# Six groups of attention outputs turned by VectorE in 32x32 blocks and moved between SBUF quadrants, in place of TensorE's transposes, under a new written order

## The chip, the core and the metric

The kernel runs on one core of a Trainium2 chip. A core has engines that run side by side, each through its own list of instructions, strictly in order: TensorE (PE; its weight loads are listed apart as PEld), VectorE (DVE), ScalarE (ACT), GpSimd (POOL) and SyncE (SP), which here only issues transfers. An engine stops at an instruction whose semaphores are not yet up, and everything behind it in its list stops with it. SBUF is the working memory of 128 partitions (four quadrants of 32), PSUM the small memory that TensorE writes into. The metric is device time in microseconds; lower is better.

## What is computed

The reference is linear attention with a feature map, followed by a soft mixture of experts:

```python
proj = einsum('bhsd,df->bhsf', x, w_phi);  proj -= max(abs(proj), -1)
phi(x) = concat([exp(proj), exp(-proj)], -1)               # 256 features, for q and k
kv, z  = einsum('bhsf,bhsd->bhfd', k_p, v), sum(k_p, 2)
out    = einsum('bhsf,bhfd->bhsd', q_p, kv) / (einsum('bhsf,bhf->bhs', q_p, z) + 1e-6)
# 8 batches x 8 heads x 576 tokens x 64;  x = out as 4608 tokens x 512
logits = x @ phi                                           # 32 slots: 8 experts x 4
d      = softmax of logits over all tokens;   slot_input = d.T @ x
slot_out[e] = relu(slot_input[e] @ w1[e]) @ w2[e]          # w1 512x1024, w2 1024x512, each expert
y      = softmax of logits over slots @ slot_out
```

All is float32. The matrix `x` never goes to memory: its tiles stay in SBUF until their part of `slot_input` has been added up.

## The kernel before, in words

**Attention.** The batches go in four pairs (`bp`), a pair of one head is a unit `u` (32 units of nine tiles of 128 tokens). For four tiles at a time (`b`, 72 of them), `proj` multiplies K and Q by `w_phi` into PSUM; VectorE takes maxima (`kmax`, `qabs`), ScalarE the exponentials (`kneg_exp`, `kpos_exp`, `qpos`, `qneg`), GpSimd scales V (`vals`), and TensorE adds up `kv` (`kvmm`). Then `num` multiplies Q's features with `kv`, three tiles at a time, VectorE combines the two halves (`scale`, `comb`, `recip`) and GpSimd divides (`divide`) into a tile `xc[n]` of 128 tokens x 4 x 512.

**A group.** When all eight heads of a pair are divided, two tiles `xc[n]` are full, n = 0 to 5 for the first three pairs; these are the six groups of the title. For each, the logits need `x` turned so that the 512 features lie on the partitions. Before, TensorE did it: task `turn` is four 128x128 transposes into a PSUM bank (line 741), four such tasks in a group, each followed by `xcopy` (line 745), which copies the bank to SBUF on ScalarE or VectorE, two and two. `logits` (line 424) then multiplies with `phs`. Behind it follow `gmax`, `gexp`, `dturn`, `dcopy`, `slotsum` and `update`, which keep a running softmax over tokens and its sum. The last pair's groups (`fturn`, `fxcopy`, `flogits`) have code of their own and come at the end of attention.

**The order.** All of that is a list of tasks. The string `ORDER` has one letter for each task, in the order in which they are written into the engines' lists; `Plan.run` checks that each task's inputs are written earlier and hands out buffers. No scheduler reorders anything afterwards. A letter's place is no time: two engines meet only where one waits for the other.

**Transfers.** SP issues all of them in one list: `xs` (K and Q, 512 KB, three buffers), `vt` (V, 325 KB, two buffers), and the 64 expert weights `wt` (512 KB each). Where SBUF is not yet needed for attention, weights come early: `room` gives the number of weight slots in each stretch of memory, 30, 33, 39, 42, 43 and 49 before; the first 30 are free from the start, the others come free as pools are closed (`ends`), and the last 15 weights reuse slots. Each transfer counts up one of eight semaphores (DMAHW0 to 7 below), in turn, and the program makes a transfer wait for the one that used its semaphore eight transfers earlier, so at most eight are in flight.

**The tail.** After attention the final groups' tasks (`z...`), the experts' first and second layer (lines 848 and 943) and the combination with the outputs (lines 972 to 976) follow, all by TensorE in a written order.

Of the kernel before, what the change touches and what calls it, by code (L numbers as in the profile page):

```python
# [9 lines left out]
F32 = mybir.dt.float32  # L10
# [6 lines left out]
B, H, S, D = 8, 8, 576, 64  # L17
FE = 128
NBP = B // 2
# [4 lines left out]
G = 4  # L24
# [20 lines left out]
BUFS = {'xs': 3, 'kf': 3, 'vs': 2, 'vt': 2, 'qf': 3, 'un': 2, 'xT': 4, 'xc': 2}  # L45
# [4 lines left out]
def room(bufs):  # L50

    parts = [bufs["xs"] * XW * 4, bufs["kf"] * 4096 + bufs["vs"] * 2624 + bufs["vt"] * 2624,
             bufs["qf"] * 4096 + 2 * 1056 + 512, bufs["un"] * 2368, (bufs["xc"] + 1) * G * DM * 4]
    return [int(n) // 4096 for n in np.cumsum([TOP - bufs["xT"] * 2048 - sum(parts)] + parts)]


class Plan:
# [43 lines left out]
    "abbccdeafdebgbehiejefechigcjdklfmbgdnoelhimjfajkegmhijcpnoclfdmqlrhisgmfjktharujnovmvkbdicnogpcjdwmgwflrjhirqvaw"  # L101
    "mxfysbkrkdtnomlhizvnocAwgpvjcjwflmdqbrAArvkshimnoltfwckvdgnojrwfrgdkyjahimzlhivnocwqvpcgbdjmgdflrAfwAhimsjklnotr"
    "hiyAmkcjvnopgwcjbdavmxgzflArdqjmwlAfaAkvrwhisynorhizmtkgcjnovvjpwcblfxdmAqrwAAfsrkgmvhitlnojwkvchwajnoyrblrdiqmv"
    "vgwkzjcdpwfmdrgynoAsrfjkmhilAathiznoAcgvjcvblfxAwmxqdAAwrgpkjsfmnolhirtvmvkwdnorwghijrvyzmAcpjwvcwAbflxyAhrazfAd"
    "imkAlgBnojdBqcCgCjsBbBdatmlCkvjwrnoChirvgfjmhiDkpAnocEwFvcwkflmbhrxqxdimGgsnojBflBtCaxchCjykdiBnozBgCfjmvhwrClpr"
    "vdimDwgvkjwnocEFcblqadHxHIrJIKksfKnoltLmqyAdAgAhirfjmgkhicpjnovscbfvxtwmlwrzflAhrvAAdimwgvhyjrwkdiajrnozvgkmjvcp"
    "nowwcAblfyhAmzqdirlgmkjsfAahrxtnoxmjkvdicAnovApwAgcGlfjhwmlqrJdirfvgmkwjsknoradnotbchijvywcblfxgvmxqjdrwpdhimvgr"
    "kzwAsmkMgylftrnozLAhiAcnojvcbdjaxwmglfAvrqApjwmkshiArfvtnowmdkMyNvhirwgljrvnojmvczwwpcyAbxlaAzArdkAlmfAnoBhiBgCc"
    "jCfkdBqdBmCgfjshinoajrlxCAbmktDphivvnocwEgwjclfFrbqrvdmwgBsfBkmktCCjdhiBvnoOajBhiyxCcClrwflrnovNzdmkwhiDgnojpcEq"
    "vGwcFblgsHHrItdmyKIjfzlhiKAdkaxALgmAnoqvJrfMjmgvkwhiwAscnoApctblAxdrjGrgvfwmkdhilrgjvajmvkwnoOPfrjNnomvhicwwPpyc"  # L110
    "yzbdkAlmfdgrnojzqJmlAajhixsAfrAOhimtkcnovvpwcgbdjlmgfrwqjdrvAklaAmhixwjnosfchitgmkvbjfxwrlxhrpyvnowmkvczdiAnowqc"
    "dyAAglmfjshirfLatbrkvgmzvkAwnodMrnApjglohicvjqwcwdmsygAfhirtfrPvkjwmaxjkdblgrjlnomzhivcpnoAvwcwAlfyAhmqdirzdgmAN"
    "ksjnoABaxgtbBCjcfCAhivjBwdBCmCrlfplrkvhimvnoDknocEqwcgblFjwBfsBCrtmjkvCwHflBnorIhCrqvJmdiGwBdKCvgwhiDjkgnocEysFc"
    "bpzLxAHaArItlmKdknomAfygjvhirwfzAravkdmlhijOgcnowqApAcvbdjmwgsfrfltrlkPymvhijwhajnoxdirkvmgznovjcGpwcblfAdmqlrks"
    "gmhijwfLAnoarytxhmAkdijcnovvpzgcwAlfjwmqdrdgArAksgmMhivtnowfljcvkyjwrnojlrzJqdmAvkvMcwAnowsgycpAhilNtrQzrAvAwmOR"
    "jlRSmvkPSqwRfRSNhirkTSvsnomUwtORApRSyQrnoVVSRvrSTvwzwARUArASyRPQvzyRwSzWASWWAyTzAXXQXYYUZYZ0WZ001223145367186794"
    "525435985658++-Q++*//=-=<>*!>!!!-*>")
# [15 lines left out]
def tile_kernel(ctx: ExitStack, tc, xT, vv, w, phi, w1, w2, cst, out):  # L133
# [13 lines left out]
    stacks = {k: ExitStack() for k in ("x", "c", "u", "q", "v", "mm", "h", "zl", "num")}  # L147
# [6 lines left out]
    def pool(k, name, **kw):  # L154
        return stacks[k].enter_context(tc.tile_pool(name=name, **kw))
# [10 lines left out]
    xp = pool("x", "xp", bufs=BUFS["xs"], side="right")  # L166

# [253 lines left out]

    def slotmm(ps, kc, t, stop=True):
# [224 lines left out]
    def spin(x):  # L647
# [3 lines left out]
                     kb0=1, kb1=1, qb0=1, qb1=1, pkv=1, kvs=2, psn=2, mo=2, mk=6, mh=1, eq=3, dn=3, lT=3, de=2,  # L651
# [10 lines left out]
    for b in range(NB + 2):  # L662
        def task(kind, engine, cost, fn, key, bank, **k):
            add(kind, key, engine, cost, lambda: fn(key), at=4 / 3 * bank, **k)
# [8 lines left out]
        for p, (b_, u, t0, t1) in enumerate(pieces):  # L673
            if b_ == b:
# [6 lines left out]
                task("kvmm", PE, 0.233 * n + 0.215 * mid, kvmm, p, b, after=[("kpos_exp", b), ("vals", p)] + ([("kvmm", p - 1)] if p else []),  # L681
# [8 lines left out]
    for s in range(NK):  # L690
# [44 lines left out]
        for i, group in enumerate(groups):  # L735
# [17 lines left out]
        def logits(m, xTs=xTs, got=got, groups=groups):  # L753
# [3 lines left out]
        task(f + "logits", PE, 0.225 * len(groups), logits, m, mode="s",  # L757
             after=[(f + "xcopy", (m, i)) for i in range(len(groups))], get=hold("logits", m),
             put=[("xT", (m, i)) for i in range(len(groups))], lat=0.22)
# [43 lines left out]
    ends = [("x", [("proj", NB + 1), ("weight", nslot[0] - 1)]),  # L803
# [7 lines left out]
    last("zopen", 1, None, 0.0, lambda: zopen("r"), after=[("zopen", 0), ("close", 1)], lat=0.0)  # L811
# [238 lines left out]
```

## Time and profile before

| | |
|---|---|
| median of 3 runs | 338.7 us (338.18 to 339.12) |
| the profiled execution | 339.44 us, of which the span from first to last instruction is 337.3 us |
| TensorE | busy 325.8 us (97% of the span) |
| VectorE | 243.8 us (72%) |
| ScalarE | 234.4 us (69%) |
| GpSimd | 168.3 us (50%) |
| transfers | 74.10 MB, 220 GB/s mean |

Attention lasts to about 268 us, the end of the slot sums to 280 us, the experts and outputs to the end. Groups 0 and 1 are turned between 73 and 90 us, 2 and 3 between 137 and 152 us, 4 and 5 between 205 and 216 us. Busy time of matmuls is modelled and overlaps; how much time a stretch of TensorE's work takes is read from the starts in the chain of waits.

### The profile page before, as it was taken

To read this page: it belongs to the slowest core of one execution; us is meant where nothing else is said; L and a number is where in the kernel's file an instruction comes from. 1 tells how busy PE (TensorE), PEld (TensorE's weight loads), DVE (VectorE), ACT (ScalarE), POOL (GpSimd) and SP (SyncE) were. 2 spreads that over 40 slices of the span, in tenths; PEclk is the share of its full clock that TensorE was granted. 3 is DMA by queue.
4 is the path that set the end of the run, shared out by engine and by line. 5 is a ranking of instruction groups with operands and counts; after the bars stand their busy time and mean duration, and the time that the engine had idled before them with its cause. 6 is when DMAs were issued, how large, how long until landed. Compare 5 with 4: busy or idle time off the path is not lost.

```text
span 337.3 us, 16424 instructions
## 1 busy us (share of the span) xinstructions
PE 325.8 (97%) x6955; PEld 274.7 (81%) x6955; DVE 243.8 (72%) x683; ACT 234.4 (69%) x680; POOL 168.3 (50%) x353
## 2 busy tenths in 40 slices
PE   8999999999999999999999999999999999999982
PEld 4899998999979999998899999979998745355750
DVE  1478887786979888778898977778998552716642
ACT  2899988968886996887788987867886241205541
POOL 1645766863547667642877785248593520240000
PEclk9999999999999999999999999999999999999997
DMA  6646366553755784465557845233618859994987
GB/s 232 176 134 227 104 211 226 203 189 117 286 166 166 230 290 172 173 224 164 167 177 253 277 176 183 67 145 127 230 45 309 311 202 386 411 409 194 391 338 301
DMA packets 22409, 74.10 MB, mean 220 GB/s; under 512 B 2496, under 2 KB 2880, under 8 KB 22336
## 3 DMA queue, kind: packets, MB, share of 16 engines
q1 hardware_dynamic: 22336, 73.05, 60.6%
q8 instruction: 55, 0.90, 1.1%
q14 instruction: 18, 0.15, 0.1%
HBM read 63.60 MB, written 9.44 MB: 217 GB/s over the span
## 4 chain that ended last, share of the span: by engine, by line
PE 91%; DVE 4%; ACT 1%; issue 1%; POOL 0%; DVEq 0%; ACTq 0%; POOLq 0%
PE kvp L318 23%; PE psn L371 21%; PE psq L271 12%; PE psk L271 10%; PE hp L848 4%; PE psx L741 4%; PE yp L943 4%; PE psl L424 3%; PE pso L972 2%; PE pss L463 2%; PE psw L190 1%; DVE o L973 1%; PE pss L566 1%; PE psd L456 1%; PE psh L910 1%
## 5 line engine op out<-in xcount | busy, mean ns | idle before, releaser
L291 POOL TENSOR_TENSOR vs<-vt,mk 128x520 f32<-128x520 f32 (+3 forms) x128 | 91.6, 732 | 70.1 <-ACT mk L280 52.3
L318 PE MATMUL kvp<-vs,kf 128*64 128x65 f32 (+1 forms) x2304 | 92.5, 229 | 0.0
L318 PEld LDWEIGHTS kvp<-vs,kf 128*64 128x64 f32 x2304 | 81.5, 138 | 7.1 <-issue 2.3
L371 PE MATMUL psn<-kvs,qf 128*64 128x65 f32 x2304 | 80.3, 223 | 0.7 <-issue 0.6
L371 PEld LDWEIGHTS psn<-kvs,qf 128*64 128x64 f32 x2304 | 73.6, 138 | 3.8 <-issue 1.7
L271 PE MATMUL psq<-xs,wd 64*128 64x128 f32 x576 | 75.8, 280 | 0.1
L271 PE MATMUL psk<-wd,xs 64*128 64x128 f32 x576 | 75.7, 280 | 0.1
L271 PEld LDWEIGHTS psq<-xs,wd 64*128 64x128 f32 x576 | 67.6, 187 | 3.1 <-issue 1.5
L271 PEld LDWEIGHTS psk<-wd,xs 64*128 64x128 f32 x576 | 67.2, 187 | 3.0 <-issue 1.5
L276 DVE TENSOR_REDUCE mk<-psk 128x4 f32<-128x512 f32 x72 | 48.4, 676 | 13.6 <-PE psk L271 8.1
L333 DVE TRANSPOSE_TENSOR_REDUCE mts<-psq 128x16 f32<-128x512 f32 x72 | 50.7, 707 | 6.6 <-PE psk L271 3.6
L302 ACT ACTIVATE kf<-psk 128x512 f32<-128x512 f32 x72 | 42.6, 592 | 17.2 <-DVE mk L276 7.5
L338 ACT ACTIVATE qf<-psq 128x512 f32<-128x512 f32 x72 | 42.4, 594 | 8.0 <-DVE dn L398 2.6
L382 DVE TENSOR_TENSOR un<-psn,eq 128x195 f32<-128x195 f32 x96 | 33.1, 351 | 18.3 <-PE psn L371 9.6
L413 POOL TENSOR_TENSOR xc<-un,dn 128x256 f32<-128x256 f32 x64 | 39.3, 616 | 13.5 <-DVE dn L398 11.0
L341 ACT ACTIVATE qf<-psq 128x512 f32<-128x512 f32 x72 | 43.2, 603 | 0.5 <-DVE mts L333 0.5
L305 ACT ACTIVATE kf<-psk 128x512 f32<-128x512 f32 x72 | 42.5, 596 | 0.5 <-DVE mk L276 0.4
L387 DVE TENSOR_TENSOR un<-psn,un 128x195 f32<-128x195 f32 x96 | 32.9, 349 | 1.0
L349 ACT ACTIVATE mh<-mts 32x36 f32<-32x36 f32 x128 | 29.5, 230 | 5.4 <-DVE mts L333 3.4
L355 DVE TENSOR_REDUCE eq<-mh 32x9 f32<-32x36 f32 x128 | 26.3, 205 | 1.5
L279 ACT ACTIVATE mk<-mk 128x4 f32<-128x4 f32 x72 | 15.1, 210 | 12.4 <-DVE mk L276 10.9
L973 ACT COPY o<-pso 128x512 f32<-128x512 f32 x20 | 11.4, 597 | 8.9 <-PE pso L972 8.9
(130 smaller groups left out, 346.0 us busy)
## 6 DMA issues: line engine op xcount, KB each, us to landing
wt<-w SPq DMA_DIRECT2D x64, 512.0 KB, 5.9
xs<-xT SPq DMA_DIRECT2D x36, 512.0 KB, 4.3
vt<-vv SPq DMA_DIRECT2D x32, 325.0 KB, 3.2
out<-o SPq DMA_DIRECT2D x17, 512.0 KB, 4.2
out<-o SPq DMA_DIRECT2D x2, 256.0 KB, 4.0
xs<-xT SPq DMA_DIRECT2D x2, 128.0 KB, 2.6
cs<-cst SPq DMA_DIRECT2D x1, 128.5 KB, 2.9
wd<-w SPq DMA_DIRECT2D x1, 64.0 KB, 2.1
```

Source lines behind the costliest of these rows:

```text
L271: nc.tensor.matmul(ps, l, r, start=True, stop=True)
L276: nc.vector.tensor_reduce(km[b][:, 2], kx[b], axis=AX, op=ALU.max, apply_absolute_value=True)
L291: nc.gpsimd.tensor_tensor(vs[b][:, :, place(b, u, t, o):place(b, u, t, o) + n], v[:, t + o:t + o + n].unsqueeze(1).broadcast_to([128, 2, n ...
L302: nc.scalar.activation(kf[b][:, 1], kx[b], AF.Exp, scale=-1.0)
L305: nc.scalar.activation(kf[b][:, 0], kx[b], AF.Exp)
L318: nc.tensor.matmul(ps[f:f + FE // 2, pn, o:o + m], kf[b][:, pn, NT * u + t - 4 * b, f:f + FE // 2], v2[:, pn, at:at + m], start=(t == 0 an ...
L333: nc.vector.tensor_reduce(mts.rearrange("p r j -> p j r")[:, o:o + 4], qx[b].rearrange("p j (r t) -> p (j r) t", t=32), axis=AX, op=ALU.ma ...
L338: nc.scalar.activation(qf[b][:, 0], qx[b], AF.Exp)
L341: nc.scalar.activation(qf[b][:, 1], qx[b], AF.Exp, scale=-1.0)
L371: nc.tensor.matmul(ps[64 * f:64 * f + 64, j, pn], q2[:, pn, 64 * f:64 * f + 64], kv[:, pn, b2], start=True, stop=True)
L382: nc.vector.tensor_tensor(un[u][:, CH * c:CH * c + CH], nx[s][:, :, 0], e[:, 1].unsqueeze(2).broadcast_to([128, CH, 65]), op=ALU.mult)
L413: nc.gpsimd.tensor_tensor(x[:, :, h * D:(h + 1) * D], un[u][:, a:b, 0:64], dn[u][:, a:b].unsqueeze(2).broadcast_to([128, b - a, 64]), op=A ...
```

## The change

For groups 0 to 5, `turn` and `xcopy` are replaced by two tasks. `xturn` (four in a group, on VectorE) turns all 32x32 blocks of one 128x512 tile of `xc[n]` and writes them to a tile `yb`, sorted by the quadrant they belong to. `xmove` (four in a group, on SP, each four transfers of 32 partitions x 2 KB = 64 KB) carries quadrant i of `yb` to the free places i of `xTb`, from quadrant i to every quadrant q. Each of the four `xmove` needs all four `xturn`. `logits` reads `xTb` in place of the copied banks. `yb` and `xTb` exist once each: the next group's `xturn` waits until the transfers of this one have read `yb`, and its `xmove` until `logits` has read `xTb`.

The two tiles take 16 KB of each partition, and `xc` has three buffers instead of two (8 KB more), so `room` now gives 24, 28, 31, 37, 40, 41 and 49 weight slots: 24 from the start, four more when the new pool is closed behind group 5. `kvmm` 4 waits for the eight warming matmuls in the list. `ORDER` is new from the first letter to the last. The final groups keep TensorE's transposes.

```diff
-BUFS = {'xs': 3, 'kf': 3, 'vs': 2, 'vt': 2, 'qf': 3, 'un': 2, 'xT': 4, 'xc': 2}
+BUFS = {'xs': 3, 'kf': 3, 'vs': 2, 'vt': 2, 'qf': 3, 'un': 2, 'xT': 4, 'xc': 3}
...
-    parts = [bufs["xs"] * XW * 4, bufs["kf"] * 4096 + bufs["vs"] * 2624 + bufs["vt"] * 2624,
+    parts = [2 * G * DM * 4, bufs["xs"] * XW * 4, bufs["kf"] * 4096 + bufs["vs"] * 2624 + bufs["vt"] * 2624,
...
-    "abbccdeafdebgbehiejefechigcjdklfmbgdnoelhimjfajkegmhijcpnoclfdmqlrhisgmfjktharujnovmvkbdicnogpcjdwmgwflrjhirqvaw"
...
+    "bccfaeeedfbeeadhggihicfclhjkmdgfnjmhjelbobjkanimpdcekgiondbecrfrlmqdlojhgjfstghmikivmjnwocfcrajvplqwudrvmbgmdksw"
...
+    yp_ = pool("y", "yp", bufs=1, side="right")
...
+    def xturn(n, j):
+
+        if j == 0:
+            yb[n] = yp_.tile([128, 4, KC, G, 32], F32, tag="y", name="yb")
+        nc.vector.transpose(yb[n][:, :, :, j].rearrange("p q k a -> p k q a"),
+                            xc[n][:, j].rearrange("p (k q a) -> p k q a", k=KC, q=4))
+
+    def xmove(n, i):
+
+        if i == 0:
+            xTb[n] = yp_.tile([128, 4, KC, G, 32], F32, tag="xTb", name="xTb")
+        for q in range(4):
+            nc.sync.dma_start(xTb[n][32 * q:32 * q + 32, i], yb[n][32 * i:32 * i + 32, q])
...
+                     after=[("kpos_exp", b), ("vals", p)] + ([("kvmm", p - 1)] if p else []) + [("spin", i) for i in range(NSPIN) if p == 4],
...
-        for i, group in enumerate(groups):
+        for i in range(0 if final else 4):
+            task("xturn", DVE, 0.62, lambda key, n=n: xturn(n, key[1]), (n, i), after=[("divide", (u, c))], get=["yb"] * (i == 0))
+        for i in range(0 if final else 4):
+            task("xmove", SP, 1.6, lambda key, n=n: xmove(n, key[1]), (n, i), after=[("xturn", (n, 3))], get=["xTb"] * (i == 0), put=["yb"] * (i == 3), lat=2.5)
+        for i, group in enumerate(groups if final else ()):
...
-                slotmm(ps, group[0][0], {j: xTs[kc, j] for kc, j in group}, stop=group is groups[-1])
+                slotmm(ps, group[0][0], {j: xTs[kc, j] if final else xTb[m[0]][:, :, kc, j] for kc, j in group}, stop=group is groups[-1])
...
-    ends = [("x", [("proj", NB + 1), ("weight", nslot[0] - 1)]),
+    ends = [("y", [("logits", (2 * NBP - 3,) + tuple(range(KC))), ("weight", nslot[0] - 1)]), ("x", [("proj", NB + 1)]),
```

Three places show how the engines' lists change. Line numbers of the changed kernel are 1 higher than before for `proj`, `vals`, `kvmm`, `num`, `scale` and `comb`, 17 higher from `slotmm` to `update`.

**TensorE at group 0's logits.** Names: `psx` is a bank of transposes, `psl` the logits, `kvp` and `psn` the products of `kvmm` and `num`, `psk` and `psq` those of `proj`. Before:

```order
L741 MATMUL psx<-cs,xc 128x128 x8
L318 MATMUL kvp<-vs,kf 64x65 x12
L371 MATMUL psn<-kvs,qf 64x65 x24
L318 MATMUL kvp<-vs,kf 64x65 x4
L424 MATMUL psl<-xT,phs 32x128 x16
```

Now, with the semaphores that an instruction waits for:

```order
L372 MATMUL psn<-kvs,qf 64x65 x11
L319 MATMUL kvp<-vs,kf 64x65 [waits Pool_49]
L319 MATMUL kvp<-vs,kf 64x65 x11
L441 MATMUL psl<-xTb,phs 32x128 [waits DMAHW3_49,DMAHW4_49,DMAHW2_49,DMAHW5_49,DMAHW1_49,DMAHW6_49,DMAHW0_49,DMAHW7_49,DVE_49,PE_49]
L441 MATMUL psl<-xTb,phs 32x128 x15
L272 MATMUL psq<-xs,wd 128x128 [waits DVE_49,PE_49]
```

The sixteen transposes of the group (two rows of eight before) are gone, and the first matmul of the logits waits for ten semaphores, eight of them of transfers, where before it waited for one at most.

**SP at group 0.** The transfers of `xmove` stand in SP's list between the loads of attention:

```order
L179 DMA xs_1707<-xT 128x1024 [waits DMAHW3_49,PE_49]
L437 DMA xTb_1709<-yb_1613 32x512 [waits DMAHW4_49,DVE_49]
L437 DMA xTb_1709<-yb_1613 32x512
L437 DMA xTb_1709<-yb_1613 32x512 [waits DMAHW6_49]
L437 DMA xTb_1709<-yb_1613 32x512 [waits DMAHW7_49]
```

Sixteen of them stand in a row, of which these are the first four, with the load ahead of them. Without numbers, and with what stands behind:

```order
L183 DMA vt<-vv 128x650
L179 DMA xs<-xT 128x1024 x2
L437 DMA xTb<-yb 32x512 x16
L183 DMA vt<-vv 128x650
L179 DMA xs<-xT 128x1024 x3
```

The first waits for VectorE (the fourth `xturn`), and V and three loads of K and Q queue behind all sixteen.

**VectorE at group 3, whose turning starts while group 2's logits are due.** Names: `un` are the unscaled outputs, `gm` the maximum of group 2's logits, `mk` and `mts` the maxima of K and Q:

```order
L388 TENSOR_TENSOR un<-psn,un 128x195 [waits DVE_49] x2
L429 STREAM_TRANSPOSE yb<-xc 128x4x4x32 [waits DMAHW4_49,DMAHW5_49,DMAHW3_49,DMAHW6_49,DMAHW2_49,DMAHW7_49,DMAHW1_49,DMAHW0_49]
L453 TENSOR_REDUCE gm<-psl 128x1 [waits PE_49]
L454 TENSOR_TENSOR low_138<-gm,low_137 128x1 [waits DVE_49]
L277 TENSOR_REDUCE mk<-psk 128x4
```

A block transpose now stands ahead of the maxima and waits for group 2's transfers to have read `yb`; before, this place held no instruction that waits for a transfer.

More of the change, by code (lines that the diff above doesn't have):

```diff
@@ L146, in tile_kernel @@
     pmo = ctx.enter_context(tc.tile_pool(name="pmo", bufs=1, space=PSUM))
-    stacks = {k: ExitStack() for k in ("x", "c", "u", "q", "v", "mm", "h", "zl", "num")}
+    stacks = {k: ExitStack() for k in ("y", "x", "c", "u", "q", "v", "mm", "h", "zl", "num")}
     def bank3(label, shape, name):
@@ L680, in tile_kernel @@
                      get=["vs"] * (p == 0 or pieces[p - 1][0] != b), put=["mk"] * end + ["vt"] * (t1 == NT))
-                task("kvmm", PE, 0.233 * n + 0.215 * mid, kvmm, p, b, after=[("kpos_exp", b), ("vals", p)] + ([("kvmm", p - 1)] if p else []),
+                task("kvmm", PE, 0.233 * n + 0.215 * mid, kvmm, p, b, after=[("kpos_exp", b), ("vals", p)] + ([("kvmm", p - 1)] if p else []) + [("spin", i) for i in range(NSPIN) if p == 4],
                      get=["pkv"] * (t0 == 0), put=["kf", "vs"] * end, mode="c", lat=0.25)
@@ L810, in tile_kernel @@
     last("zopen", 0, None, 0.0, lambda: zopen("l"), after=[("qread", NB - 2), ("qread", NB - 1)], lat=0.0)
[L811 removed]
+    last("zopen", 1, None, 0.0, lambda: zopen("r"), after=[("zopen", 0), ("close", 2)], lat=0.0)
     opens = [("zopen", 1)]
```

41 lines of the change are left out of this document (21 added, 20 removed), and 2 rows, old and new, of the table LETTERS.

## The prediction

> **What bounds the kernel now.** I read the page's busy times first, then the chain of waits, then busy time by stretch, and last who waited for whom.
>
> ```profile
> PE 325.8 (97%) x6955; PEld 274.7 (81%) x6955; DVE 243.8 (72%) x683; ACT 234.4 (69%) x680; POOL 168.3 (50%) x353
> PE 91%; DVE 4%; ACT 1%; issue 1%; POOL 0%; DVEq 0%; ACTq 0%; POOLq 0%
> ```
>
> TensorE is busy for 97% of the span, and 91% of the chain that ended last lies on it. A busy matmul row can be a stalled one, so the stretches have to be looked at. Columns: PE, PEld, DVE, ACT, POOL, clock, share of the transfer engines, GB/s.
>
> ```profile
> 10.00:70.00 60.00, 59.41 (x1522) 56.35 (x1520) 46.80 (x127) 51.48 (x153) 37.85 (x77) 1.00 0.54 178
> 72.00:137.00 65.00, 64.79 (x1578) 59.89 (x1576) 54.11 (x148) 52.15 (x158) 40.31 (x84) 1.00 0.60 208
> 137.00:204.00 67.00, 67.00 (x1616) 61.89 (x1612) 56.29 (x160) 56.84 (x173) 42.41 (x89) 1.00 0.60 203
> 204.00:253.00 49.00, 49.00 (x1134) 44.43 (x1131) 40.11 (x117) 38.94 (x118) 28.89 (x63) 1.00 0.39 134
> 230.00:240.00 10.00, 10.00 (x254) 9.56 (x252) 9.36 (x27) 7.52 (x24) 6.47 (x14) 1.00 0.54 182
> 280.00:300.00 20.00, 20.00 (x187) 8.19 (x189) 8.54 (x41) 3.20 (x7) 5.24 (x8) 1.00 1.01 404
> ```
>
> In the 241 us of the first four rows TensorE is busy for 240.2, at full clock; VectorE is at 78 to 84%, in the fullest ten microseconds at 94%. The weight loads, PEld, are at 90 to 94% too, so this is work and not waiting. Each piece taken from TensorE's list in attention shortens attention, as long as nothing else has to be waited for. After 280 us the transfer engines are full; that is looked at below.
>
> **What the change removes.** 96 transposes, sixteen in each of six groups. The rows of the chain, of the same eight in weight loads, and of the transposes and copies by form:
>
> ```profile
> 85.47 1.02 PE psx L741 x8
> 87.58 1.02 PE psx L741 x8
> 73.34 0.86 PEld L741 LDWEIGHTS psx<-cs,xc 128*128 128x128 f32 x8
> L741 PE MATMUL psx<-cs,xc 128*128 128x128 f32 x120 | 16.8, 280 | 0.0
> L745 DVE COPY xT<-psx 128x512 f32<-128x512 f32 x16 | 10.9, 682 | 4.7 <-PE psx L741 4.5
> L745 ACT COPY xT<-psx 128x512 f32<-128x512 f32 x17 | 10.1, 592 | 7.7 <-PE psx L741 7.6
> L333 DVE TRANSPOSE_TENSOR_REDUCE mts<-psq 128x16 f32<-128x512 f32 x72 | 50.7, 707 | 6.6 <-PE psk L271 3.6 <-PE psq L271 1.3 <-ACT qf L338 0.9
> ```
>
> The 280 ns of one transpose overlap its neighbours. In the chain eight take 1.02 us, 0.128 us each, the switch to the next work included; by the weight loads alone eight take 0.86 us, 0.108 each. So 96 are worth 10.3 to 12.2 us on the path that sets the end; I take 12.2. The copies go from engines off that path: twelve of ScalarE (12 x 0.592 = 7.1 us) and twelve of VectorE (12 x 0.682 = 8.2 us).
>
> **What it adds to VectorE.** 24 block transposes of 128x512, which no row shows. The nearest are the copy of the same size (0.682 us) and the turned maximum, which reads as much (0.707). From below, ScalarE's copy, 0.592; from above, two passes, one for the reading and one for the turned writing, 1.41 us. I take 0.69 as for the copy, 24 x 0.69 = 16.6 us, so VectorE carries 8.4 us more. By pair of groups, 72 to 137 us: 54.1 us less four copies (2.7) plus eight transposes (5.5) makes 56.9 us, in a stretch that shrinks from 65 to 60.9; 93% there, and (56.3 + 2.8) of 62.9, 94%, in the next. That is the fullest ten microseconds of before as an average. VectorE still fits, and it frees PSUM banks for TensorE (`scale`, `comb`) with less to spare: 0 to 4 us of new waits, I take 1. The Trainium skill, "VectorE: DVE Perf Modes", The three transpose paths and Rules for kernel authors, speaks against the change: a 128x128 block belongs on TensorE (390 ns) if PSUM will do. By its 311 ns for a 128x128 set of blocks on VectorE (both figures for bf16), an estimate for the 96 is 29.9 us in place of 16.6; the rule does not ask which engine is full, and here it is TensorE.
>
> **What it adds to the transfers.** 96 of 64 KB, sixteen in a group, in SP's list.
>
> ```profile
> L242 SPq DMA_DIRECT2D wt<-w x64: 327/424/1762, 24.6 to 297.3; - x64
> L178 SPq DMA_DIRECT2D xs<-xT x36: 327/328/959, 3.1 to 238.1; - x36
> wd<-w SPq DMA_DIRECT2D x1, 64.0 KB, 2.1
> phs<-phi SPq DMA_DIRECT2D x1, 64.0 KB, 2.6
> xs<-xT SPq DMA_DIRECT2D x36, 512.0 KB, 4.3
> wt<-w SPq DMA_DIRECT2D x64, 512.0 KB, 5.9
> SPq L242 <- DMA wt<-w: 8.5, 10, 1.4
> SPq L178 <- PE psk L271: 102.1, 26, 10.1
> 98.67 0.70 PE psn L371 x24
> 99.37 0.93 PE kvp L318 x32
> 102.32 1.08 PE kvp L318 x32
> ```
>
> One issue takes 0.33 to 0.42 us and about 0.05 to the next, so sixteen take 6.1 to 7.6 us; transfers of 64 KB land in 2.1 to 2.6 us. From the end of the fourth block transpose to `logits` that makes 8.2 to 10.2 us, which TensorE has to fill with other work. It does, nearly. In the list of group 0 there stand, from that transpose to the logits, fifteen tiles of `kvmm` (0.27 us each by the last row), four `num` (0.70 each) and three `proj` (two of them lie between 100.30 and 102.32 us of the chain, 1.0 each): 9.9 us, less the transpose itself, 0.7, makes 9.2. Group 4 has fourteen tiles, 8.9 us, and group 2, whose four block transposes stand in a row at the start of its count, about 8 after them. Groups 1, 3 and 5 have 13 us and more. So three of six groups stand at the edge, between 2 us too late and 1 us to spare: 0 to 6 us in all, I take 2. When `logits` is late, everything on TensorE behind it is late by as much; VectorE's first transpose of groups 3 and 5, which waits for the same transfers, holds up `gmax` and the maxima behind it at the same moment, which is no second price.
>
> The loads behind the sixteen are the other queue. SP had time: loads of K and Q waited 102.1 us for TensorE to free a buffer, so they were early. In group 0, V and the first of three `xs` now leave about 7 us after the block transposes and land 4.3 later, some 11.3 us after them, when `proj` 28, which reads it, stands 3 us of TensorE's work behind the start of the logits (2 for these, 1 for `proj` 27), 12.2 us after them. This fits with about a microsecond to spare; I take nothing, and put it with the 6 us of the upper end, since the same lateness decides both.
>
> The Trainium skill, "DMA: Bandwidth & Descriptors", Bandwidth, has a rule against such sizes: batch to 1 MiB, 64 KB being dominated by descriptors at 0.95 us of transfer time. Its fixed cost of about 2 us (Anatomy of one DMA) agrees with the 2.1 and 2.6 us of the rows above. If sixteen times 0.95 us ran one after the other, an estimate by that page is 17.2 us to the landing of the last, against the 10.2 above.
>
> **Semaphores on TensorE.** The first matmul of `logits` waits for up to ten semaphores.
>
> ```profile
> L741 PEldq EVENT_SEMAPHORE  x13: 51/51/51, 75.2 to 267.0; - x13
> ```
>
> An extra wait is an instruction of 51 ns in TensorE's own list. Nine of them in six groups are 2.8 us at most, nothing if they pass while the array still works on what was issued; thirteen such (0.7 us) go with the transposes. I take 1.5.
>
> **The tail.** Six weights fewer are loaded early (24 instead of 30), four of them again before attention ends, so 28 stand where 30 stood, 37 where 39, 49 where 49.
>
> ```profile
> 276.93 20.72 SPq L242 DMA_DIRECT2D wt<-w  x21
> 299.85 5.32 PE yp L943 x96
> 312.94 1.45 PE yp L943 x48
> ```
>
> The last 21 weights are issued from 276.9 us; 21 x 0.524 MB at the 404 GB/s of the stretch 280 to 300 us are 27 us, so the last lands at about 304, and the second half of the second layer, which reads it, runs from 312.9 on. Now the last stretch begins some 10 us earlier with 23 weights, 30 us, and ends at about 297, with the reader at about 303 and its last expert later still. Two weights more than before are 2.6 us, and the slack is 9. Nothing, then, as long as that slack lasts; the bound is 2.6 us.
>
> **Sum.** Against the profiled execution, 339.4 us (span 337.3 and 2.1 around it): 339.4 - 12.2 + 1 + 2 + 1.5 = 331.7. The median of the runs shown is 0.7 below that execution, so I forecast 331 us. Least: 12.2 gone and nothing paid, 326.5. Most, with all mechanisms as forecast: 339.4 - 10.3 + 4 + 6 + 2.8 + 2.6 - 0.7, just under 344; all upper ends together are unlikely, and 338 holds most of it.
>
> **Rivals.** *All of it is hidden*: no new waits but the semaphores, 339.4 - 12.2 + 1 - 0.7 = 327.5. For it: a bound engine relieved of work, with ScalarE 7 us lighter. Against it: three groups at the edge.
>
> *The transfers are late* (the slower side): they share the transfer engines with weights and loads and land as those do. Place: `logits` on TensorE. By the semaphores at most eight are in flight, and SP's 8.5 us of waits for earlier weights show that this binds, so with a landing time L the ninth leaves at L, the sixteenth 7 x 0.38 later, and the last lands 2L + 2.7 us after the block transposes. At L = 5.9, the weights' time, that is 14.5 against 9.2 us of cover: 5.3 in each of the three groups, and little in the others, 16 to 18 us, for 346 us in all. It decides from about L = 4.9, where the three groups pay 3.3 each and eat the gain up with the other terms. For it: the weights' 5.9. Against: 64 KB landed in 2.1 and 2.6, and around these groups the engines are at 0.60, not full.
>
> *VectorE becomes the bound*: a block transpose of 1.41 us brings 54.1 - 2.7 + 11.3 = 62.7 us into a stretch of 60.9. At no more than 94% filling it needs 66.7, so each of three pairs loses 1.7 us against before instead of winning 4: 344 us. It decides from 1.2 us each. For it: the strided turned writes. Against: the turned maximum, which also passes 128x512 through the same turning, takes 0.707.
>
> *The new order*, where it need not differ, is worth something of its own, either way; the old one left TensorE no idle time, so there is nothing to win in attention beyond the terms above.
>
> **Chances.** The forecast 0.50, all hidden 0.24, late transfers 0.15, VectorE 0.08, other 0.03. About 0.3% (1.0 us) is what a measurement of this kernel tells from no change. Faster, below 337.7: nearly all of the first two and a third of the late transfers (L of 3 to 4.5), 0.77. Same 0.07. Slower 0.16. The range goes from 326 to 340: it leaves out VectorE's case and the worse half of the late transfers. The forecast's own range is 327 to 338.
>
> **What would show it.** No transposes on TensorE between 60 and 240 us; a block transpose at 0.6 to 0.75 us in the rows; 64 KB landing in 2 to 3 us; waits of `psl` for transfers of 0 to 2 us in groups 0, 2 and 4 and none elsewhere; VectorE at 90% or more from 70 to 240 us; TensorE's first layer starting at about 272 us instead of 279.8, and the same 57 us from there to the end. The prediction is wrong if the rows for `psl` show waits of 3 us or more, if `psk` waits for `xs`, or if the tail is longer than before.

## The result, and the profile after

| | before | the change | forecast |
|---|---|---|---|
| median, us | 338.8 (338.18 to 339.12) | 355.0 (353.25 to 357.07) | 331.0 (326 to 340) |
| ratio to before | | 1.048, 95% interval 1.042 to 1.055 | 0.977 |
| profiled execution: span, us | 337.3 | 354.0 | |
| TensorE's first layer starts, us | 279.8 | 297.4 | about 272 |
| from there to the end, us | 57.5 | 56.6 | 57 |

The change is 16 us slower where 8 us faster was forecast, and all of it lies ahead of the two layers. Medians here and below are over all runs of a kernel; ratios leave out runs that the chip did in its slower state, so the two can differ by some tenths of a per cent. The page of the change, its busy times and its chain of waits by engine and by line:

```profile
PE 321.7 (91%) x6859; PEld 267.9 (76%) x6859; DVE 249.1 (70%) x695; ACT 230.2 (65%) x668; POOL 168.5 (48%) x353
PE 53%; DVE 12%; DMA 12%; SPq 9%; issue 6%; POOL 5%; ACT 1%; DVEq 0%; POOLq 0%; ACTq 0%
PE kvp L319 14%; PE psn L372 14%; SPq L437 8%; DMA wt<-w 8%; PE psk L272 7%; PE psq L272 7%; PE psl L441 3%; POOL vs L292 2%; DVE yb L429 2%; PE yp L964 2%; DMA xTb<-yb 2%; DVE mk L277 2%; PE pso L993 2%; DMA xs<-xT 1%; DVE un L383 1%
```

TensorE had 91% of the chain before and has 53% now; SyncE's queue (SPq), which had none, has 9%, of which 8 are the issues of `xmove` (line 437). The transfers have 12%, but 8 of these are expert weights (`wt`) behind the slot sums, a stretch that did not get longer; the pieces (`xTb`) are 2. The windows show where (columns as in the prediction; four of seven windows, and the sum of all):

```profile
10.00:90.00 80.00, 74.76 (x1895) 70.33 (x1891) 62.68 (x165) 66.81 (x194) 47.12 (x96) 1.00 0.53 169
90.00:100.00 10.00, 8.38 (x150) 7.74 (x152) 5.18 (x14) 3.23 (x13) 2.87 (x5) 0.66 0.75 248
160.00:170.00 10.00, 6.79 (x120) 5.89 (x122) 4.27 (x13) 5.11 (x21) 2.19 (x4) 0.83 0.70 230
230.00:240.00 10.00, 7.11 (x122) 4.96 (x120) 5.55 (x16) 3.61 (x13) 2.54 (x6) 0.83 0.65 218
sum 287.00, PE 265.44 PEld 237.24 DVE 221.97 ACT 208.51 POOL 160.94; mean PE 37.92 PEld 33.89 DVE 31.71 ACT 29.79 POOL 22.99
```

Of the 287 us from 10 to 297 TensorE is busy for 265.4 and idle for 21.6; before, in the 241 us of four such rows, it was idle for 0.8. The granted clock, 1.00 in those rows, is 0.66 and 0.83 on average in the stretches with the longest waits. What stands behind the stalls shows in the wait list (us in all, times, longest):

```profile
POOL vs L292 <- DMA vt<-vv: 18.9, 8, 9.5
PE psl L441 <- DMA xTb<-yb: 11.6, 3, 5.5
DVE yb L429 <- DMA xTb<-yb: 6.0, 2, 3.2
```

The row of the block transposes (busy us, ns of one, and VectorE's idle time before them):

```profile
L429 DVE STREAM_TRANSPOSE yb<-xc 128x512 f32<-128x512 f32 x24 | 15.6, 685 | 6.8 <-DMA xTb<-yb 6.0
```

The view of the tile `xTb`, with the issue's ns (least, median, most) and the time to landing:

```profile
L437 SPq DMA_DIRECT2D xTb<-yb x96: 507/589/1928, 76.8 to 254.1; - x96
DMA to landing us min/median/max: 1.9/2.5/7.7
```

And SyncE's timeline around group 0 (start, length, what):

```profile
76.81 12.71 SPq L437 DMA_DIRECT2D xTb<-yb  x16
89.65 0.50 SPq L183 DMA_DIRECT2D vt<-vv  x1
90.25 5.70 SPq L179 DMA_DIRECT2D xs<-xT  x3
```

The block transpose takes 0.685 us and the landing 2.5 us, both as forecast. The issue does not: its median is 0.589 us where 0.33 to 0.42 was taken, and sixteen take 12.71 us where 6.1 to 7.6 was taken. So the pieces are late for `logits` by up to 5.5 us, and V and the next blocks of K and Q, which stand behind the sixteen on SyncE, are late too.

### The profile page after: what moved, and what is told of

Read it like the earlier page. It is cut to its first block, busy times and chain, and to the rows that moved or that the text cites. A ratio compares the mean times of both kernels' runs of the same rounds, so it can differ in the third digit from the quotient of the medians.

```text
span 354.0 us, 16386 instructions
## 1 busy us (share of the span) xinstructions
PE 321.7 (91%) x6859; PEld 267.9 (76%) x6859; DVE 249.1 (70%) x695; ACT 230.2 (65%) x668; POOL 168.5 (48%) x353
## 4 chain that ended last, share of the span: by engine, by line
PE 53%; DVE 12%; DMA 12%; SPq 9%; issue 6%; POOL 5%; ACT 1%; DVEq 0%; POOLq 0%; ACTq 0%
PE kvp L319 14%; PE psn L372 14%; SPq L437 8%; DMA wt<-w 8%; PE psk L272 7%; PE psq L272 7%; PE psl L441 3%; POOL vs L292 2%; DVE yb L429 2%; PE yp L964 2%; DMA xTb<-yb 2%; DVE mk L277 2%; PE pso L993 2%; DMA xs<-xT 1%; DVE un L383 1%
## 5 line engine op out<-in xcount | busy, mean ns | idle before, releaser
L319 PE MATMUL kvp<-vs,kf 128*64 128x65 f32 (+1 forms) x2304 | 86.0, 229 | 3.2 <-POOL vs L292 1.6
L319 PEld LDWEIGHTS kvp<-vs,kf 128*64 128x64 f32 x2304 | 79.0, 138 | 7.5 <-POOL vs L292 4.1
L372 PE MATMUL psn<-kvs,qf 128*64 128x65 f32 x2304 | 81.3, 226 | 1.9 <-issue 1.3
L272 PE MATMUL psk<-wd,xs 64*128 64x128 f32 x576 | 78.1, 285 | 2.2 <-issue 1.3
L272 PE MATMUL psq<-xs,wd 64*128 64x128 f32 x576 | 78.7, 285 | 0.0
L272 PEld LDWEIGHTS psk<-wd,xs 64*128 64x128 f32 x576 | 69.2, 192 | 6.3 <-issue 2.1
L272 PEld LDWEIGHTS psq<-xs,wd 64*128 64x128 f32 x576 | 69.3, 192 | 5.7 <-ACT qf L342 2.1
L339 ACT ACTIVATE qf<-psq 128x512 f32<-128x512 f32 x72 | 42.6, 596 | 10.8 <-PE psn L372 2.8
L429 DVE STREAM_TRANSPOSE yb<-xc 128x512 f32<-128x512 f32 x24 | 15.6, 685 | 6.8 <-DMA xTb<-yb 6.0
L441 PE MATMUL psl<-xTb,phs 128*32 128x128 f32 x192 | 8.3, 324 | 13.1 <-DMA xTb<-yb 11.6
```

Source lines behind the costliest of these rows:

```text
L272: nc.tensor.matmul(ps, l, r, start=True, stop=True)
L319: nc.tensor.matmul(ps[f:f + FE // 2, pn, o:o + m], kf[b][:, pn, NT * u + t - 4 * b, f:f + FE // 2], v2[:, pn, at:at + m], start=(t == 0 an ...
L339: nc.scalar.activation(qf[b][:, 0], qx[b], AF.Exp)
L372: nc.tensor.matmul(ps[64 * f:64 * f + 64, j, pn], q2[:, pn, 64 * f:64 * f + 64], kv[:, pn, b2], start=True, stop=True)
```

## The experiments

**The cost of an issue by itself.** A kernel that computes nothing of the reference: sixteen transfers of a kind, issued one behind the other (the shapes in a word each; `a` and the targets lie in SBUF, `w` in memory).

```diff
+ thin:   32 x 2 KB, a -> SBUF     tall:   128 x 512 B, a -> SBUF    wide: 32 x 4 KB, a -> SBUF
+ memory: 32 x 2 KB, w -> SBUF     loads:  512 KB, w -> SBUF         halves: thin, by SyncE and ScalarE in turn
```

> Transfers alone, no work of the reference: six series of sixteen in SP's list, each series waiting for the one before. thin: SBUF to SBUF, 32 partitions of 2 KB, as in the change; tall: SBUF to SBUF, 128 partitions of 512 bytes; memory: from memory, 32 partitions of 2 KB; wide: SBUF to SBUF, 32 partitions of 4 KB; halves: as thin, issued in turn by SP and ScalarE; loads: from memory, 128 partitions of 4 KB, 512 KB each. In the changed kernel one issue of the thin kind took 0.59 us against 0.33 to 0.43 of the loads. If the shape of 32 partitions sets it, thin, memory and wide take 0.59 and tall and loads 0.33 to 0.43. If SBUF as the source sets it, memory is at 0.4 and tall at 0.59. If it is only that issues stand back to back, all series are near 0.6. If issues of two engines go side by side, halves takes half of thin's time from first to last.

Rows of its views by tile: the issue in ns as above and, on the line behind it, the time to landing.

```profile
L34 SPq DMA_DIRECT2D thin<-a x16: 569/590/597, 12.8 to 22.3; - x16
DMA to landing us min/median/max: 2.0/2.0/2.0
L48 SPq DMA_DIRECT2D memory<-w x16: 401/419/427, 45.3 to 52.3; - x16
DMA to landing us min/median/max: 1.8/2.0/2.1
L59 SPq DMA_DIRECT2D loads<-w x16: 327/328/433, 87.4 to 116.3; - x16
```

`thin` is the change's form, SBUF to SBUF, 32 rows of 2 KB; `memory` the same 64 KB out of memory; `loads` the 512 KB of the loads. From SBUF to SBUF an issue costs 0.59 us, from memory to SBUF 0.42 and 0.33. Twice the bytes from SBUF took 0.588 and 128 rows of 512 B 0.599, so from SBUF to SBUF neither size nor shape sets it here. A source in SBUF is not enough: the kernel's results, 512 KB from SBUF to memory, take 0.33 us to issue (median of 19, before as in the change). The 0.59 is shown for SBUF on both sides only. Halves given to SyncE and ScalarE went side by side, eight in 4.96 and in 5.29 us. No issue on SyncE took over 0.61 us in these series (the 18 results in a row at this kernel's end took 0.35 to 1.27); in the change two of group 0's sixteen take 1.9 us. What those two wait for was not found.

**Later logits, and loads ahead.** First hypothesis: TensorE's wait for the pieces is the price, so reading them later mends it. A table shifts tasks in the written order by letters (CHAIN is the logits and what follows from them up to the slots' sums):

```diff
+LATER = {(kind, n): 50 for kind in CHAIN for n in (0, 2, 4)}
```

> The changed kernel with the logits of groups 0, 2 and 4, and the tasks that follow from them (gmax, gexp, gsum, dturn, dcopy, slotsum), 50 letters later in the written order, which is some 6.7 us of TensorE's work (1822 letters for 244 us). If the sixteen issues of a group (10.8 to 12.7 us) make these three logits late, their waits (5.5, 3.2 and 2.9 us) go, and with them the slow clock after them (3.4 + 1.7 + 1.7 us): 355 - 11.6 - 6.8 = 337 us; up to 341 if the loads behind the sixteen then hold TensorE up. If VectorE is the bound, or the new order itself is what costs, it stays at 352 to 357 us.

Measured 369.8 us (ratio 1.088, 1.079 to 1.097). TensorE no longer waits for pieces, but for K and Q (`xs`, 6.5 us), for `un` (7.5) and for `vs` (5.8). With the loads shifted as well:

```diff
+LATER.update({("vload", n): -90 for n in (11, 20, 28, 30)})
+LATER.update({("load", n): -90 for n in (14, 24, 33, 35)})
```

> As the kernel with later logits, and besides four loads of V and four of K and Q that stand behind the sixteen transfers of groups 0, 2, 4 and 5 go 90 letters ahead, so most of them in front of these. If the loads behind the transfers are a second price (GpSimd waited 9.5 us for V in group 0, TensorE 5 us behind the load at 255 us), 2 to 5 us less than with the later logits alone: 333 to 337 us. If not, the same time as that.

Measured 375.6 us (1.106, 1.098 to 1.115). Both expectations missed. Each kernel moved much at once, so they show that the wait for the pieces was not the whole price, and little more.

**The new order with TensorE's transposes.** The transposes and copies of before, put into the new order by hand, up to 30 letters behind the block transposes' places (a is the second of these in a group).

```diff
+place["turn"][g + 2:g + 4] = a + 14, a + 16
+place["xcopy"][g:g + 4] = a + 8, a + 12, a + 26, a + 30
```

> The new written order with TensorE's transposes and copies back in it (two and two, in the places from the group's first two letters on), without block transposes and transfers; buffers and early weights as in the change (24, three xc; the two tiles are not used). If the transfers are the cause, the time is that of the kernel before, 338 to 342 us: the 12.2 us of transposes are back, the 18 us of waits gone. If the new order or the 24 weights cost on their own, 348 us or more.

Measured 362.6 us (1.069, 1.061 to 1.077); GpSimd waited 18.9 us for the slot sums to free a tile `xc`. That acquits nothing: the places chosen by hand may cost as much as what they were to test. From here on, the order of the computing engines stays untouched wherever it can.

**No transfers, transfers that nobody reads, and half of them elsewhere.** In the first the block transposes fill two tiles in turn and the logits read those; in the second the sixteen are issued and land, but the logits read `yb`; the other two only change who issues.

```diff
 no_moves:      def xmove(n, i):  xTb[n] = yb[n]
 moves_unread: -xTb[m[0]][:, :, kc, j]     +yb[m[0]][:, :, kc, j]
 two_act:      -nc.sync.dma_start(...)     +(nc.sync if q < 2 else nc.scalar).dma_start(...)
 two_pool:                                 +(nc.sync if q < 2 else nc.gpsimd).dma_start(...)
```

> The 96 transfers are left out and the logits matmuls read the block-transposed tile where VectorE wrote it, so the logits get the quadrants in the wrong places; order, VectorE's transposes and every other instruction stay. Theory (the sixteen issues, 10.8 to 12.7 us on SyncE, make the logits late and hold the loads behind them): the three waits for the transfers (11.6 us), VectorE's two for the free tile (6.0 us) and the loads' lateness go, TensorE's idle time from 10 to 297 us falls from 21.6 us to under 5 us, and the low clock behind the stalls goes: 329 to 334 us. Rival (the new order, or the 24 block transposes on VectorE, cost the time by themselves): stays over 343 us.

Measured 334.6 us (0.987, 0.983 to 0.991), 0.6 above its range and far below the rival's: the transfers cost 20.4 us of the change's 355.0; order and block transposes alone make a kernel 1.3% faster than before.

> The sixteen transfers of each group are issued and land as in the change, but nothing reads what they bring: the logits matmuls read the block-transposed tile itself (wrong quadrants). This parts the two harms of the transfers. If TensorE's own wait for the pieces is nearly all of it: 330 to 336 us. If the loads and the tiles queued behind the sixteen on SyncE are a harm of the same size: 338 to 346 us, with waits for xs, vt or wt in place of psl. Rival (order or VectorE): over 350 us.

Measured 353.3 us (1.044, 1.035 to 1.053). With TensorE's wait for the pieces gone, 1.7 us come back of 20.4, inside the intervals. Over 350 us was put down to the order or VectorE; `no_moves` has both, so it is the unread transfers. Waits that stand in the place of the one for pieces:

```profile
POOL vs L292 <- DMA vt<-vv: 14.6, 5, 8.6
PE psk L272 <- DMA xs<-xT: 5.5, 1, 5.5
```

SyncE's timeline without transfers (`no_moves`):

```profile
76.55 0.33 SPq L183 DMA_DIRECT2D vt<-vv  x1
76.93 0.42 SPq L179 DMA_DIRECT2D xs<-xT  x1
83.05 0.33 SPq L179 DMA_DIRECT2D xs<-xT  x1
88.30 0.33 SPq L179 DMA_DIRECT2D xs<-xT  x1
```

And with unread ones (`moves_unread`):

```profile
77.31 11.72 SPq L437 DMA_DIRECT2D xTb<-yb  x16
89.16 0.50 SPq L183 DMA_DIRECT2D vt<-vv  x1
89.76 1.70 SPq L179 DMA_DIRECT2D xs<-xT  x3
```

V, due at 76.55 us, is issued at 89.16, and the first block of K and Q, due at 76.93, at 89.76. Both are some 12 us late, by the length of the sixteen (0.4 us of the 12.6 and 12.8 this run was behind already). The unread transfers cost time at least here.

> Half of the sixteen issues of a group go to ScalarE's queue, nothing else is edited. Theory: SyncE spends 8 x 0.59 = 4.7 us, the two series go side by side, the last piece lands 5 + 2.5 = 7.5 us after the first issue, under the 8 to 9.2 us of cover, so the psl waits fall from 11.6 to under 2 us and the loads come 6 us earlier; but ScalarE pays 48 x 0.6 = 29 us in its own stream, of which some comes through: 335 to 345 us. Rival (landing time or the order counts, the issues do not): 352 us or more with the psl waits as they are.

Measured 367.2 us (1.084, 1.078 to 1.090), a miss. SyncE's eight take 6.05 us. ScalarE's eight of group 0 go out from 75.96 to 87.46 us, scattered between its own activations, because its queue too is in order. First and last row of them in ScalarE's timeline:

```profile
75.96 1.48 ACTq L437 DMA_DIRECT2D xTb<-yb  x2
...
86.95 0.51 ACTq L437 DMA_DIRECT2D xTb<-yb  x1
```

TensorE's wait for the pieces is longer than in the change (11.6):

```profile
PE psl L441 <- DMA xTb<-yb: 13.7, 3, 7.1
```

> The same with GpSimd in ScalarE's place (168 us busy of 354, so it has more room). Theory: 333 to 342 us if GpSimd's issue costs about what SyncE's does; if it costs 1 us or more each, 8 of them last as long as sixteen on SyncE did and the psl waits stay at 8 to 12 us, 350 us. Rival (the order counts): 352 us or more.

Measured 441.1 us (1.304, 1.296 to 1.312), a miss far beyond the range. GpSimd's issues as a group:

```profile
L437 POOL DMA_DIRECT2D xTb<-yb x48 | 25.8, 537 | 84.6 <-issue 83.0 <-DMA xTb<-yb 0.8 <-DVE un L383 0.7
```

And in the wait list:

```profile
PE kvp L319 <- POOL vs L292: 61.0, 12, 13.4
```

The row says 0.537 us each, but 83.0 us of unexplained idle time stand ahead of the 48, 1.7 us for each, and TensorE waits 61 us for GpSimd's `vs`. The Trainium skill, "DMA: Bandwidth & Descriptors", Issuing engines are not separate DMA queues, says that issuing on several engines only saves the sequencer's issue time, which is usually small beside the transfer. Here it is the large part: 12.71 us of issuing ahead of a landing of 2.5. The Trainium skill, "Perfetto Trace Analysis", DMA Optimizations, says that where issuing is the bottleneck, balancing over the engines may help. In these two runs it did not: ScalarE's issues come as late as its own activations let them, and what GpSimd waits for in its 83.0 us no run shows.

**Count or bytes, and the order on SyncE alone.** All unread unless said. Eight issues a group; sixteen of a quarter of the bytes; and sixteen whole ones behind or between the loads that come due (SyncE's own list only). `loads_first` is the last of these with the pieces read, which takes group 0's logits back with them.

```diff
 half_unread:  -for q in range(4):   +for q in range(2):
 small_unread: -dma_start(xTb[n][32 * q:32 * q + 32, i], yb[n][32 * i:32 * i + 32, q])
               +dma_start(xTb[n][32 * q:32 * q + 32, i, 0], yb[n][32 * i:32 * i + 32, q, 0])
 loads_first*: +LATER = {("xmove", 0): 75.4, ("xmove", 1): 41.5, ("xmove", 2): 51.4, ("xmove", 3): 35.5, ("xmove", 7): 13.5,
               +         ("xmove", 13): 23.5, ("load", 24): -33, ("load", 33): -20, ("vload", 30): -21}
```

> Eight of a group's sixteen transfers, and nothing reads them (the logits matmuls read the block-transposed tile, wrong quadrants): 0 transfers ran 334.6 us, 16 ran 353.3 us. Theory (the loads of vt and xs stand behind the transfers on SyncE and come later by the time that the issues take): 8 x 0.65 = 5 us instead of 12 us of lateness; with the load's slack of a few us most of the loss goes: 336 to 344 us. Rival (any reader or writer of the block tile, not the count, makes the difference): 350 us or more.

> All sixteen, unread as before, but each moves a quarter of the bytes (32 rows of 512 B, 16 KB). Theory (it is the number of issues on SyncE): as with whole ones, 348 to 356 us, 10 to 12 us for sixteen issues. Rival (the bytes in the 16 DMA engines delay the loads' landing): 336 to 342 us.

> All sixteen at full size, unread, but on SyncE the loads of vt and xs that come due meanwhile stand ahead of the transfers or between eights and fours of them (groups 0, 1, 2, 3, 4 and 5); the other engines' order is that of the change. Theory (loads queued behind the sixteen): their lateness falls from 12.6 us to under 5 us and most of the loss goes: 336 to 344 us, vt waits under 5 us. Rival (the transfers cost by traffic, or SyncE's total time counts wherever they stand): 350 us or more.

> The same places on SyncE with the transfers read as in the change (nothing left out): group 0's logits go behind its transfers, some 30 letters of the written order later. Theory: the loads are in time, TensorE's wait for the last pieces stays at 5 to 12 us in all, as in the change: 342 to 350 us, between the change and before. If the two waits add without cover: 355 us or more. Rival (order or VectorE at fault): 352 us or more with no wait for loads.

| issues in a group | bytes each | place on SyncE | median, us | ratio, 95% interval |
|---|---|---|---|---|
| 0 | | | 334.6 | 0.983 to 0.991 |
| 8 | 64 KB | as in the change | 340.7 | 0.998 to 1.012 |
| 16 | 16 KB | as in the change | 352.0 | 1.028 to 1.043 |
| 16 | 64 KB | as in the change | 353.3 | 1.035 to 1.053 |
| 16 | 64 KB | loads first | 347.3 | 1.018 to 1.029 |
| 16, read | 64 KB | loads first | 356.1 | 1.047 to 1.058 |

The count decides, as forecast: a quarter of the bytes brings 1.3 us, inside the intervals; half the issues bring 12.6. But loads first wins only 6 us with nobody reading, between its two ranges, and nothing with the pieces read, as the second of its ranges had it. What is late in `loads_first`:

```profile
PE psl L459 <- DMA xTb<-yb: 11.3, 4, 4.0
DVE yb L447 <- DMA xTb<-yb: 7.7, 2, 3.9
POOL vs L310 <- DMA vt<-vv: 5.9, 5, 2.3
```

The wait for V fell from 18.9 to 5.9 us. The middle row is a third coupling: there is one tile `yb`, so VectorE's first block transpose of the next group waits until SyncE has issued, and the engines have moved, the last sixteen; with the loads ahead these end later still.

**The block tile.** Two tiles `yb` in turn. Beside whole pieces they fit only with fewer weight tiles held ahead, so the pieces are the quarter-size ones, unread, whose bytes made 1.3 us.

```diff
-yb[n] = yp_.tile([128, 4, KC, G, 32], F32, tag="y", name="yb")
+yb[n] = yp_.tile([128, 4, KC, G, 32], F32, tag="y", name="yb", bufs=2)
```

> Two block tiles alone: the transfers (unread, quarter size) stand where the change has them, ahead of the loads. Against small_unread's 352.0 us: if the loads queued behind are the larger part, 346 to 352 us; if VectorE's wait for the block tile is the larger part, 336 to 343 us.

> SyncE's order of loads_first_unread, sixteen unread quarter-size transfers (their bytes made 1 us of difference), and two block tiles in turn instead of one, so that VectorE's next block transposes don't wait for the transfers of the group before. If the loss of 353.3 against 334.6 us is the loads behind the sixteen plus VectorE's wait for the block tile: 335 to 341 us, with no wait of VectorE for the transfers. If something else of the transfers costs too: 345 us or more.

| unread | as in the change | loads first |
|---|---|---|
| one block tile | 352.0 | 347.3 |
| two block tiles | 342.9 (1.006 to 1.013) | 336.0 (0.982 to 0.995) |

Both together give 336.0 us, against 334.6 with no transfers at all: with those two couplings undone the sixteen issues (of a quarter of the bytes) cost 1.4 us, inside the intervals, as long as nobody reads them. The second tile is worth 9.1 us alone, loads first 4.7 (6.0 against the whole pieces that it was run with), both 16.

**The block transposes on VectorE.** `no_moves` without them; the logits read `xc`.

> Neither transfers nor block transposes: the logits matmuls read the attention outputs as they stand (not transposed, wrong logits). Against no_moves (334.6 us) this prices the 24 block transposes on VectorE. If crowding of VectorE (16.4 us of work put in) makes the 5 us that no_moves lacks against TensorE's saved 12.2 us: 328 to 331 us. If the new order does: 333 to 336 us.

Measured 334.2 us (0.983 to 0.991), 0.4 under `no_moves`: what the 24 block transposes cost is lost in the intervals. Why those two kernels gain only 4 to 5 us from 12.2 us taken off TensorE is seen at the end of attention. Windows of `no_moves`:

```profile
230.00:240.00 10.00, 10.00 (x260) 9.25 (x257) 9.70 (x30) 8.91 (x30) 6.02 (x16) 1.00 0.95 338
240.00:250.00 10.00, 8.45 (x136) 6.25 (x132) 5.48 (x19) 4.12 (x12) 5.82 (x13) 0.83 0.60 223
```

The first layer's matmuls in it:

```profile
L866 PE MATMUL hp<-wt,phs x128: 592/592/617, 276.6 to 291.7; 128*32 128x512 f32 x128
```

To 240 us TensorE is full, and the relief shows: 560 of the 576 matmuls of `psq` have started by then, which before had by 250. From there, where the last groups follow one another, TensorE is idle at times, the window's mean clock is 0.83, and 7 us of the chain, 245.9 to 252.9, lie on VectorE and GpSimd. The last matmul of `psl` starts at 267.9, 4.7 us earlier than before, the first layer at 276.6, 3.2 us earlier, not 12.

**The mend.** Whole kernels, nothing left out: loads first and two block tiles, paid for with two weight tiles fewer held ahead; then the same with the logits' chain later by the time that the pieces miss; then with a fourth tile `xc`, two more weight tiles fewer.

```diff
 mend:       -parts = [2 * G * DM * 4, ...   +parts = [3 * G * DM * 4, ...
 mend_later: +LATER.update({(kind, n): d for kind in CHAIN for n, d in ((0, 45), (1, 4), (2, 42), (4, 32), (5, 6))})
 mend_xc4:   -'xc': 3                        +'xc': 4
```

> A whole kernel, nothing left out: loads ahead of or between the transfers, two block tiles (two weight tiles fewer are held ahead in exchange), and the logits behind their transfers in the written order. loads_first_two_tiles without readers ran 336.0 us; the logits there ran at 86.0, 152.5 and 215.5 us, where the pieces land at some 91.6, 158 and 219.8 us, so 16 us of waits for pieces in groups 0, 2 and 4 less what is made up: 342 to 352 us, against 356.1 us of loads_first.

> The same, with the logits and what follows them up to the slots' sums 45, 4, 42, 32 and 6 letters later in groups 0, 1, 2, 4 and 5 (about the 5.6, 0.3, 5.5, 4.3 and 0.5 us by which the pieces land late), nothing left out. If the three couplings (loads, block tile, pieces) are all: no wait of TensorE for pieces over 2 us, 335 to 341 us, about before's 338.8 or a little under. If the later chain holds the divided outputs too long (three tiles of them): 343 to 355 us with GpSimd or VectorE waiting for xc.

> As mend_later with a fourth tile for the divided outputs (four weight tiles fewer held ahead than in the change), nothing left out. If the hold on those tiles is what mend_later still pays: 3 us or more below it; if the weights held ahead count in the layers: 2 to 5 us above it.

They ran 355.8 us (1.044 to 1.059), 352.0 (1.033 to 1.045) and 343.0 (1.005 to 1.017). The first misses its range: with loads and tile mended, TensorE waits for the pieces again, 11.8 us, and the time is the change's. In the second that wait is 0.5 us, and 3.1 more before group 1's logits, which the list puts down to a weight though these matmuls read pieces. The later chain also holds the divided outputs longer; the wait list of `mend_later`:

```profile
PE psn L391 <- DVE un L407: 6.2, 6, 2.0
DVE un L402 <- POOL xc L433: 6.0, 4, 3.5
PE psl L460 <- DMA wt<-w: 3.1, 1, 3.1
```

The fourth tile `xc` brings 9 us, to 3.8 us above the 339.2 that before ran beside these. None beats before. The only ones that do leave the transfers out or unread.

## Why the prediction was wrong, point by point

- **What the change removes: the instructions right, their worth not.** The 96 transposes are gone. They were priced as if TensorE set the end of all of attention. `no_moves`, with VectorE's 0.4 us taken off, wins 4.6 us: after 240 us, where it was some 10 us ahead, the chain of the last groups sets the end and half of the lead is lost.
- **VectorE: right.** 0.685 us each against 0.69, and 0.4 us in all against the 1 taken. The 90% filling named as a sign did not come: VectorE is busy for 73 to 82% from 70 to 240 us, as TensorE stalls in between. By the Trainium skill, "VectorE: DVE Perf Modes", The three transpose paths, the estimate was 29.9 us (its figure is for bf16); the rows make 24 x 0.685 = 16.4.
- **The transfers: the step that failed.** "One issue takes 0.33 to 0.42 us" was read from transfers of 512 KB out of memory. From SBUF to SBUF it is 0.59, sixteen in a row take 10.8 to 12.7 us instead of 6.1 to 7.6, and in groups 0, 2 and 4 the last piece lands 12 to 14 us after the block transposes against 8 to 9.2 of cover, not 8.2 to 10.2. The three groups named are the three that wait (5.5, 3.2, 2.9 us), for 11.6 us against the 2 taken. The landing, 2.5 us, was right. The estimate from the Trainium skill, "DMA: Bandwidth & Descriptors", Bandwidth, 17.2 us to the last landing, is above the 12 to 14, and issuing, not moving, made the most of these; the page's rule is for transfers under 64 KB, its 0.95 us for loads from memory issued by GpSimd.
- **"The loads behind the sixteen … I take nothing": failed.** They were to leave about 7 us after the block transposes, with a microsecond of slack. They left 12.9 us after them (76.8 to 89.65), some 12 later than without transfers. The sign that was named, `psk` waiting for `xs`, is there with 0.6 us, and with 5.5 where nobody reads the pieces. SyncE's 102 us of waits for free buffers were read as room. They were not: a load that waits there goes in the moment its buffer is free, and in that moment the sixteen stand ahead of it.
- **"Which is no second price": right in the change, but it hides a price.** VectorE's wait for the block tile was dismissed, as falling in the same moment as the late logits. It does: its two waits (3.2 and 2.9 us) end with TensorE's for groups 2 and 4, at 164.3 and some 233.3 us. Only where the readers are away does the second tile win 9.1 us; with the pieces read it won nothing that shows (356.1 to 355.8, with two weight tiles fewer).
- **The clock was not in the sum.** After the longest stall TensorE goes on at half speed. Its chain there, logits and projections:

```profile
91.62 1.93 PE psl L441 x32
93.55 0.51 PE psq L272
94.07 0.21 PE psq L272
...
96.84 0.19 PE psk L272
97.03 0.11 PE psk L272
```

  A step of the projection takes 0.21 us until 97.03, then 0.11: 5.4 us at half speed, worth some 2.7. The two shorter waits lie in the windows of 0.83; behind the 2.9 us one the same 32 matmuls again took 1.94 us, where group 2's took 1.15. The Trainium skill, "TensorE: Matmul & The Clock Gate", What's actually happening, gives half rate after an idle window of about 3.4 us and full rate after a busy one, the windows running freely; the halving agrees, and the way back took 5.4 us here, but the 2.9 us wait was shorter than that window (TensorE's idle time goes by the modelled ends of matmuls).
- **The semaphores.** The trace has 24 extra instructions at `logits`, 51 ns in the median, which makes 1.2 us against the 1.5 taken; whether they cost time no run tells. **The tail** is as forecast, 56.6 us, though its chain now runs through weight transfers.
- **The rivals.** "The transfers are late" had the place and the sign and under half the size (346 us, 7 above before, where 16 were measured), but by landing time, from 4.9 us on, and landing was 2.5. The 0.15 it got was weighed on that row, while the row that decided, an issue from SBUF to SBUF, was not in the trace. A longer issue was: the 64 KB load `wd`, whose 2.1 us of landing the sum used, took 0.568 us to issue, at the kernel's start. The upper bound should have come from there, not from 0.42.

How the 20.4 us split among the three couplings has no single answer: taking away the readers alone wins 1.7 us, then (with quarter-size pieces) the second tile 9.1, and loads first with it 16; with the pieces read, loads first and the second tile together win nothing (355.8). Each wait, once gone, uncovers the next, since all of them follow one late queue. What stays open is the two issues of 1.9 us, and whether an order planned with 0.59 us an issue, instead of tasks shifted by hand, would bring `mend_xc4` below before.

## What to carry to other kernels

Count the issues of a queue as work of their own: sixteen small transfers from SBUF to SBUF were 11 to 13 us of SyncE's queue here, at 16 KB as at 64 KB each, and the loads that stood behind them were late by as much. A queue that waits for buffers much of the time need not have room; look where each load would go out, and what stands ahead of it in that moment. And when a late queue feeds several readers, test them together: mending one of three waits won 1 to 9 us of 20, or nothing.

## What the runs showed of the hardware that was not expected

An issue on SyncE took 0.59 us from SBUF to SBUF, for rows of 512 B to 4 KB alike, 0.42 from memory to SBUF with 64 KB and 0.33 with 512 KB, and 0.33 from SBUF to memory (512 KB results). ScalarE's took about as long (medians 0.53 and 0.60) and went beside SyncE's; with GpSimd each cost about 1.7 us of idle time of that engine beside its 0.54. A stall of 5.5 us on TensorE left it at half speed for 5.4 us more.
